# Moving the first layer's low weight parts from GpSimd to VectorE in an attention and two-MLP kernel

## The chip, the core and the metric

The kernel runs on one core of a Trainium2 chip. The core has a matrix engine (TensorE, PE in the profile), a vector engine (VectorE, DVE), a scalar engine (ScalarE, ACT), GpSimd (POOL) and a queue that issues DMAs (SyncE, SP). Each engine takes its own instructions in the order in which they were written, and waits where an operand of another engine or of a DMA isn't there yet. The metric is the device time of one execution in microseconds (us), measured in several runs; the profile is of one more execution of the same program.

## The reference

The program computes three things in a row: a linear attention with a feature map of exponentials, an MLP with a SiLU gate, and an MLP with a squared ReLU. Shapes: 4 batches, 8 heads, 576 tokens, head size 64, 128 features; then 2304 tokens, model width 512, hidden width 2048.

```python
def phi(x):
    proj = np.einsum('bhsd,df->bhsf', x, w_phi)
    proj = proj - np.max(np.abs(proj), axis=-1, keepdims=True)
    return np.concatenate([np.exp(proj), np.exp(-proj)], axis=-1)
q_p, k_p = (phi(q), phi(k))
kv = np.einsum('bhsf,bhsd->bhfd', k_p, v)
z = np.sum(k_p, axis=2)
num = np.einsum('bhsf,bhfd->bhsd', q_p, kv)
den = np.einsum('bhsf,bhf->bhs', q_p, z)[..., None] + 1e-06
x = (num / den)                       # [batch, heads, tokens, 64] -> [2304, 512]
h = x @ moe_w_in;  x = (h * (1.0 / (1.0 + np.exp(-h)))) @ moe_w_out
h = np.maximum(x @ moe2_w_in, 0.0);  out = (h * h) @ moe2_w_out
```

## The kernel before, in words

**Blocks and chunks.** The 2304 tokens are cut into 8 blocks of 288 (half a batch each). The hidden width of each MLP is cut into 16 chunks of 128. For a block i and a chunk c of layer L, `chunk` (line 871) multiplies the block's input by the chunk's input weights into a bank `h` (line 888, 12 matmuls), applies the activation on ScalarE and VectorE into tiles `a`, `gh`, `gl`, and adds the product with the chunk's output weights to four banks `o` (line 933, 12 matmuls). All 16 chunks of a block come before the next block; block 0 of layer 0 is therefore the place where each chunk's weights are used for the first time. They then stay in SBUF for the other seven blocks.

**Splits.** A matmul operand is not used as it is, but as a high part (rounded by a cast on ScalarE, `hi_act`, line 327) and a low part (the number less its high part, `lo_on`, line 331), and three products are added. Line 331 is one helper for all low parts; which engine runs it is an argument.

**Weights.** They come as float64 bits. For each half chunk (`part` 0 is the input half, 1 the output half) `w_conv` (line 394) loads 512 KB into one of three raw buffers (`wr`), takes the magnitude on ScalarE (line 408), and packs a float32 with four VectorE instructions (lines 414, 416, 420, 424) into `wc`. `w_split` (line 438) then makes the high part on ScalarE and the low part, both in the tile `w` of the chunk. In layer 0 the low part of half chunks 0 to 29 is made on GpSimd, and that of the last two on VectorE (`LP0, LP1 = 0, 2`, line 276, and line 1002). In layer 1 all are made on VectorE.

**Attention.** `keys_of` (line 479) makes the keys' features (`pk`, `kp`) and their product with the values (`pkv`, `kv`) for a batch and a pair of heads. `queries_of` (line 716) makes for half a batch and a pair of heads the projection (`pq`, evacuated to `qp`), its maximum over the 128 partitions on GpSimd (`peak`, line 763, into `qm`), the difference on VectorE (line 769), two exponentials on ScalarE (`qe`, line 781), the product with `kv` (`pn`, line 815), and the division by the denominator, whose reciprocals go through DRAM (`rr`, `rd`, `qb`). Names carry the numbers of the block and the pair: `qm1_2` is the maximum of block 1 and pair 2.

**The order.** No order is written by hand. `Plan` (line 65) plays the operations through with a cost for each and a key that says when it is wanted, and emits them in the order in which they start there: for every engine the ready operation with the least key. The costs are numbers of the program: `MM` and `MM256` (line 260) for a matmul, 450 + 6.25 S for a partition maximum (line 771), `pool(n)` (line 252) and `dve(n)` (line 248) for elementwise work on GpSimd and VectorE. A cost has no effect on the chip except through the order.

**GpSimd.** It runs a few memsets, the 32 partition maxima, and the 30 subtractions. In the program's order of GpSimd's instructions a row of kind ISA without a tile stands wherever the work turns from subtractions to maxima or back.

Of the kernel before, what the change touches and what calls it, by code (L numbers as in the profile page):

```python
# [17 lines left out]

B, H, S, D, F = 4, 8, 576, 64, 128
NTOK, DM, DFF = B * S, H * D, 2048  # L20
NP = H // 2          # pairs of heads
HB = S // 2          # tokens of a block: half a batch
NB = NTOK // HB      # blocks
NC = DFF // 128      # chunks of the hidden layer
ND = DM // 128
KT = 116             # tokens of a k tile; the last one has 112
NKT = 5
LAST = S - KT * (NKT - 1)
D1 = D + 1           # a head's values and a column of ones
RP, RN = 96, 2 * HB // 96  # L30


# [1 line left out]
    return struct.unpack("<f", struct.pack("<I", bits))[0]  # L34


# the high word of a float64, read as a float32: of float32's least and largest numbers
MIN_HI = float_of(896 << 20)
MAX_HI = float_of((1151 << 20) - 1)

# [7 lines left out]


class Buf:  # L50
    """A tile that a pool lends from its first writer to its last user."""

    def __init__(self, pool, make, unit):
        self.pool, self.make, self.unit, self.users, self.tile = pool, make, unit, 0, None


class Unit:
    """A chain of operations that shares the slots with others."""

    def __init__(self, n):  # L60
        self.n = n
# [1 line left out]


class Plan:
    """Operations in the order of the data, put by their costs into an order for the engines."""

    LAT = {"PE": 450, "SP": 150}
    DMA_LAT = 2000
# [1 line left out]
    def __init__(self, pools):  # L71
        self.ops, self.units, self.free = [], [], dict(pools)
        self.written, self.read, self.started = {"kvs": ()}, {}, set()
        self.last = {}       # pool -> [buffers to come back, pool that opens then, its size]

    def unit(self):
        u = Unit(len(self.units))
# [39 lines left out]
        return o  # L117

    def more(self, u, running):
        """The slots that unit `u` still needs beside those it holds, if it runs in its own order."""  # L120
        now = most = 0
        users = {}
        for o in u.ops:
            if o.state == 2:
                continue
            if o.state == 0 and o is not running:
                n = sum(b.pool == "t" for b in o.allocs)
                now += n
                most = max(most, now)
            for b in o.frees:  # L130
                if b.pool == "t":
                    users[b] = users.get(b, 0) + 1
                    if users[b] == b.users:
                        now -= 1
        return most

    def safe(self, o):
        """Whether the units can still end one after another once `o` has its buffers."""
        need = {}
        for b in o.allocs:  # L140
            need[b.pool] = need.get(b.pool, 0) + 1
        if any(self.free[pool] < n for pool, n in need.items()):
            return False
        n = need.get("t", 0)
        free = self.free["t"] - n
        if n and o.unit:
            for u in self.active:
                if u.n > o.unit.n:
                    break
                if u is not o.unit:  # L150
                    if self.more(u, None) > free:
                        return False
                    free += u.held
            if self.more(o.unit, o) > free:
                return False
        return True
# [100 lines left out]
    return max(600, kb * 1024 / 330.0)  # L257


MM, MM256 = 122, 109  # L260


@with_exitstack
def attention_then_two_mlps(ctx, tc, kT, qT, v, w_phi, w1, w2, out):
# [8 lines left out]
    WARM = 4  # L273
    JF, BX = 2, 1
    EW = 14
    LP0, LP1 = 0, 2
    NX, NXK = 1, 2      # batches whose queries, and keys, are multiplied as float32

    const = ctx.enter_context(tc.tile_pool(name="const", bufs=1))
    wp = ctx.enter_context(tc.tile_pool(name="wp", bufs=NC - NW))  # L280
# [5 lines left out]
    rp = ctx.enter_context(tc.tile_pool(name="rp", bufs=NRAW))  # L286
    tp = ctx.enter_context(tc.tile_pool(name="tp", bufs=NT))
    psb = ctx.enter_context(tc.tile_pool(name="psb", bufs=8, space=PSUM))
    # the space of the last chunks' weights serves the attention at the start
    early = tc.tile_pool(name="ep", bufs=NE)  # L290
    ep = [early.__enter__()]

# [15 lines left out]
    op = plan.op  # L308
# [13 lines left out]
            b.tile = b.make()  # L322
        return b.tile

    # ---- exact splits: hi has the 12 leading bits, lo the rest
    def hi_act(dst, src):
        nc.scalar.copy(out=dst, in_=src)  # L327

# [4 lines left out]
    def lo_cost(engine, n):  # L333
        return dve(n) if engine == "DVE" else pool(n)

    # ---- constants
    wbl = const.tile([128, 2, F], F32, name="wbl")
    wst_hi = const.tile([128, F], F32R, name="wst_hi")
    wst_lo = const.tile([128, F], F32R, name="wst_lo")
# [33 lines left out]
    op(T0 - 99, "ACT", 600, phi_hi, r=["wraw", "wbl0"], w=["phi_hi"])  # L373
    op(T0 - 99, "DVE", 600, phi_lo, r=["wraw", "phi_hi"], w=["phi_lo"])

    # the tensor engine's clock rises after a few microseconds of work
    blank_u = Buf("e", lambda: ep[0].tile([128, 256], F32, tag="t", name="zeros"), None)
    blank_ps = Buf("eb", lambda: psb.tile([128, 512], F32, tag="b", name="warm"), None)

# [7 lines left out]
    op(T0 - 100, "DVE", 300, zeros, w=["zeros"], bufs=[blank_u])  # L387
    op(T0 - 100, "PE", WARM * 850, warm, r=["zeros"], bufs=[blank_u, blank_ps])

    # ---- weights of a layer, chunk by chunk: [in hi, in lo, out hi, out lo].  # L390
    # They come as float64 bits: word 0 holds the low 32, word 1 the high 32.
    wch = {}

    def w_conv(layer, c, part, key):
        """float64 to float32: |x| is kept in float32's range, the exponent loses 896, and 3 bits
        of the low word follow the 20 mantissa bits of the high one."""
        n = f"{layer}_{c}_{part}"
        u = plan.unit()
        u.early = layer == 0 and 2 * c + part < EW
        raw = Buf("raw", lambda: rp.tile([128, 512, 2], I32, tag="raw", name="wr" + n), None)  # L400
        f = slot("wc" + n, u, (128, 512))

        def load():
            src = (w1, w2)[layer][c, :, part * 512:(part + 1) * 512].bitcast(I32)
            nc.sync.dma_start(out=get(raw).rearrange("p n two -> p (n two)"), in_=src)

        def mag():
            nc.scalar.activation(out=get(f), in_=get(raw)[:, :, 1].bitcast(F32), func=AF.Abs)  # L408

        def bits(i):  # L410
            t, b = get(f), get(f).bitcast(I32)
            lo, hi = get(raw)[:, :, 0], get(raw)[:, :, 1]
            if i == 0:
                nc.vector.tensor_scalar(out=t, in0=t, scalar1=MIN_HI, scalar2=MAX_HI, op0=ALU.max, op1=ALU.min)
            elif i == 1:
                nc.vector.tensor_scalar(
                    out=b, in0=b, scalar1=5, scalar2=2, op0=ALU.logical_shift_left, op1=ALU.logical_shift_right
                )
            elif i == 2:
                nc.vector.scalar_tensor_tensor(  # L420
                    out=b, in0=lo, scalar=29, in1=b, op0=ALU.logical_shift_right, op1=ALU.bitwise_or
                )
            else:
                nc.vector.scalar_tensor_tensor(  # L424
                    out=b, in0=hi, scalar=-(1 << 30), in1=b, op0=ALU.bitwise_and, op1=ALU.bitwise_or
                )

        k = ("wf", layer, c, part)
        hold = int(key) - 6 if layer else 0
        r = [(("c", 0, hold // NC, hold % NC), "h")] if layer else []  # L430
        op(key - 4, "SP", dma(512), load, r=r, w=[(k, 0)], bufs=[raw])
        op(key, "ACT", act(512), mag, r=[(k, 0)], w=[(k, 1)], bufs=[raw, f], unit=u)
        for i in range(4):
            op(key, "DVE", dve(512, i < 2), lambda i=i: bits(i), r=[(k, 1 + i)], w=[(k, 2 + i) if i < 3 else k],
               bufs=[raw, f], unit=u)
        return f, u
# [36 lines left out]
        op(key, "SP", dma(256), load, r=[(k, "d"), (("c", 0, NB - 1, max(c - 2, 0)), "h")], w=[k], bufs=[f], unit=u)  # L473
        return f, u

    # ---- keys and values of a pair of heads
    kvs = {}

    def keys_of(j, p, key, lo_engine="DVE"):
# [173 lines left out]
        ps = pkv  # L653

        def kv_mm():
            # a head's 65 columns of values and ones among 128, the others fall between the results
            for g, tiles in enumerate(groups):
                nt = KT if g < 2 else LAST
                for i, t in enumerate(tiles):
# [43 lines left out]
            op(key, "DVE", dve(4 * D1), kv_lo, r=[(K, "t"), (K, "kvh")], w=[(K, "kvl")], bufs=[ps, kv], unit=u)  # L703
        kvs[j, p] = kv

    # ---- queries of a pair of heads, half a batch
    xs = {}

    def x_buf(u):
# [6 lines left out]
    def queries_of(b, p, key, lo_engine="DVE"):  # L716
# [51 lines left out]
            f = get(pr).rearrange("p a t -> p (a t)")  # L768
            nc.vector.tensor_tensor(out=f, in0=f, in1=get(mx), op=ALU.subtract)  # L769

        op(key, "POOL", 450 + 6.25 * S, peak, r=[(Q, "pr", 0), (Q, "pr", 1)], w=[(Q, "m")], bufs=[pr, mx], unit=u)
        op(key, "DVE", dve(S), sub, r=[(Q, "m")], w=[(Q, "d")], bufs=[pr, mx], unit=u)
        hls = []
        for s in range(2):
# [48 lines left out]
            op(key, "ACT", act(HB, True), evac, r=[(Q, "n", a)], w=[(Q, "num", a)], bufs=[ps, num], unit=u)  # L823

        rb = slot("qb" + n, u, (D, 2, HB))
        # the denominators' reciprocals, spread over partitions, then one row for all of a head's
        rr = Buf("rr", lambda: sp.tile([RP, RN], F32, tag="rr", name="rr" + n), None)

        def spread():
# [35 lines left out]
        op(key, "ACT", act(HB), x_hi, r=[(Q, "x")], w=[("xh", b, p)], bufs=[x, xb])  # L865
        op(key, "DVE", dve(HB), x_lo, r=[(Q, "x"), ("xh", b, p)], w=[("xl", b, p)], bufs=[x, xb])

    # ---- the MLPs on blocks of HB tokens
    accs = {}

    def chunk(L, i, c, key):
# [108 lines left out]
            op(key, "DVE", dve(S), lo, r=[X] + [("xh", NB + i, d) for d in ps], w=[("xl", NB + i, d) for d in ps],  # L980
               bufs=[raw, xb], unit=u)

    # ---- the work in the order of the data, with keys: when it is wanted, in chunks of a block
    todo = []

    def want(key, f, *args):
        # what a block reads is declared before it, however late it is wanted
        first = key
        if f in (keys_of, queries_of):
            first = min(key, 32 * args[0] - P["qe"] - 1 if f is keys_of else 16 * args[0] - 0.5)  # L990
        if f == "key":
            first = min(key, args[1])
        todo.append((first, len(todo), key, f, args))
# [4 lines left out]
    for c in range(NC):  # L998
        def first(key, c=c):
            for part in range(2):  # L1000
                f, u = w_conv(0, c, part, key + 0.5 * part)
                w_split(0, c, part, f, u, key + 0.5 * part, "POOL" if LP0 <= 2 * c + part < 32 - LP1 else "DVE")
        want(min(T0 + P["w0"] + P["ws"] * c, c - P["we"]), "key", first, c - 1)
    for j in range(B):
        t = 32 * j
# [76 lines left out]
```

## Time and profile before

| what | value |
|---|---|
| three runs | 1100.44, 1100.52, 1101.17 us (median 1100.52) |
| profiled execution, first to last instruction (span) | 1099.0 us |
| the runs' median less that span | 1.5 us |
| PE, busy | 1016.9 us |
| DVE, busy | 619.4 us |
| ACT, busy | 549.3 us |
| POOL, busy | 117.7 us |

The page gives no other time of the profiled execution than its span; the 1.5 us are taken for what lies around it. An engine is busy while an instruction of it runs; an idle engine waits for another, and "<-" names what ended the wait. The clock column (PEclk) is the TensorE clock that was granted, as a share of full speed.

### The profile page before, as it was taken

The numbers are of one execution on the slowest core, as the hardware profiler recorded it, in microseconds if no ns is written. First come the engines' busy times: TensorE is split into PE (matmuls) and PEld (weight loads), VectorE is DVE, ScalarE is ACT, GpSimd is POOL, SyncE is SP. The second block draws the span as 40 slices with busy tenths as digits, with TensorE's granted clock in tenths as the row PEclk, the third lists the DMA queues.
The fourth block names the chain that finished last, engine by engine and source line by source line (L and its number), as shares of the span: only waits on it lengthen the run. The fifth ranks groups of instructions, "written<-read, shape, count | busy, mean of one in ns | idle before, by whom it ended". The sixth has DMA issues, their size and how long they took to land.

```text
span 1099.0 us, 19156 instructions
## 1 busy us (share of the span) xinstructions
PE 1016.9 (93%) x7424; PEld 988.3 (90%) x7424; DVE 619.4 (56%) x1248; ACT 549.3 (50%) x1369; POOL 117.7 (11%) x86
## 2 busy tenths in 40 slices
PE   7855299599999999999999999999999999999998
PEld 6624198599999999899999999999999999999998
DVE  4555389657666675678999768633333232323232
ACT  4453268566768765777766456332323232323222
POOL 2223243223000320002011000000000000000000
PEclk8967599899999999999999999999999999999999
DMA  6342335302230022424455587201001010100000
GB/s 169 101 124 69 97 95 171 96 29 60 65 78 23 23 77 56 106 89 137 131 188 159 167 283 245 85 1 45 17 28 37 9 44 1 44 1 23 1 23 22
DMA packets 67387, 88.39 MB, mean 80 GB/s; under 512 B 30816, under 2 KB 43232, under 8 KB 67296
## 3 DMA queue, kind: packets, MB, share of 16 engines
q1 hardware_dynamic: 67296, 87.17, 26.7%
q8 instruction: 58, 0.95, 0.4%
q14 instruction: 33, 0.27, 0.1%
HBM read 69.17 MB, written 17.90 MB: 79 GB/s over the span
## 4 chain that ended last, share of the span: by engine, by line
PE 75%; DMA 7%; DVE 6%; issue 4%; ACT 3%; SPq 2%; POOL 2%; ACTq 0%; DVEq 0%; POOLq 0%
PE h L888 33%; PE o L933 33%; PE pn L815 4%; DMA wr<-w 2%; PE pkv L622 2%; PE pkv L665 1%; DMA v<-v 1%; POOL qm L763 1%; DVE wc L420 1%; DVE wc L424 1%; PE pk L561 1%; SPq L503 1%; DMA rd<-rr 1%; POOL w L331 1%; SPq L731 1%
## 5 line engine op out<-in xcount | busy, mean ns | idle before, releaser
L888 PE MATMUL h<-x,w 128*128 128x288 f32 x3072 | 453.3, 297 | 32.5 <-POOL w L331 31.8
L933 PE MATMUL o<-gh,w 128*128 128x288 f32 x2048 | 457.4, 297 | 1.4 <-ACT gh L327 1.4
L888 PEld LDWEIGHTS h<-x,w 128*128 128x128 f32 x3072 | 424.9, 190 | 35.7 <-POOL w L331 33.8
L933 PEld LDWEIGHTS o<-gh,w 128*128 128x128 f32 x2048 | 345.7, 189 | 2.2 <-ACT gh L327 1.7
L933 PE MATMUL o<-gl,w 128*128 128x288 f32 x1024 | 302.9, 296 | 0.5 <-DVE gl L331 0.5
L331 DVE TENSOR_TENSOR gl<-a,gh 128x288 fp32r<-128x288 f32 x256 | 120.3, 470 | 146.5 <-ACT gh L327 145.4
L327 ACT CAST gh<-a 128x288 fp32r<-128x288 f32 x256 | 111.9, 437 | 181.4 <-PE o L933 148.0
L933 PEld LDWEIGHTS o<-gl,w 128*128 128x128 f32 x1024 | 193.5, 189 | 1.3 <-DVE gl L331 0.9
L905 DVE TENSOR_TENSOR a<-h,a 128x288 f32<-128x288 f32 x128 | 58.4, 456 | 108.1 <-ACT a L896 108.1
L896 ACT ACTIVATE a<-h 128x288 f32<-128x288 f32 x128 | 52.6, 411 | 117.3 <-PE h L888 117.1
L763 POOL PARTITION_ALL_REDUCE qm<-qp x32 | 70.3, 2216 | 326.5 <-ACT qp L756 262.5
L901 DVE SCALAR_TENSOR_TENSOR a<-a,h 128x288 f32<-128x288 f32 x128 | 57.4, 449 | 54.6 <-ACT a L894 53.6
L894 ACT ACTIVATE a<-h 128x288 f32<-128x288 f32 x128 | 53.4, 418 | 42.6 <-PE h L888 42.5
L781 ACT ACTIVATE qe<-qp 128x576 f32<-128x576 f32 x64 | 41.9, 682 | 37.4 <-DVE qp L769 30.2
L331 POOL TENSOR_TENSOR w<-wc,w 128x512 fp32r<-128x512 f32 x30 | 45.3, 1520 | 91.5 <-ACT w L327 45.4
L408 ACT ACTIVATE wc<-wr 128x512 f32<-128x512 f32 x64 | 43.3, 679 | 13.4 <-DMA wr<-w 13.0
L815 PE MATMUL pn<-qe,kv 128*65 128x288 f32 x64 | 23.8, 534 | 25.9 <-ACT qe L781 25.9
L420 DVE SCALAR_TENSOR_TENSOR wc<-wr,wc 128x512 int32<-128x512 int32 x64 | 46.5, 729 | 0.8
L424 DVE SCALAR_TENSOR_TENSOR wc<-wr,wc 128x512 int32<-128x512 int32 x64 | 45.7, 715 | 0.3
L769 DVE TENSOR_TENSOR qp<-qp,qm 128x576 f32<-128x576 f32 x32 | 26.8, 840 | 33.1 <-POOL qm L763 33.1
L594 ACT ACTIVATE ke<-pk,mx 116x128 f32<-116x128 f32 (+1 forms) x160 | 45.3, 386 | 0.0
L665 PEld LDWEIGHTS pkv<-v,kp 116*128 116x128 f32 (+1 forms) x320 | 38.0, 198 | 7.1 <-ACT kp L649 5.4
(84 smaller groups left out, 1009.8 us busy)
## 6 DMA issues: line engine op xcount, KB each, us to landing
wr<-w SPq DMA_DIRECT2D x64, 512.0 KB, 4.3
w2d<-wc SPq DMA_DIRECT2D x32, 256.0 KB, 2.9
w2f<-w2d SPq DMA_DIRECT2D x32, 256.0 KB, 3.6
qr<-qT SPq DMA_DIRECT2D x56, 144.0 KB, 3.1
v<-v SPq DMA_DIRECT2D x16, 290.0 KB
kr<-kT SPq DMA_DIRECT2D x16, 288.0 KB, 4.8
qb<-rd SPq DMA_DIRECT2D x32, 144.0 KB, 4.0
x2d<-y SPq DMA_DIRECT2D x32, 144.0 KB, 1.8
```

Of the source, the lines that this page charges most:

```text
L327: nc.scalar.copy(out=dst, in_=src)
L331: e.tensor_tensor(out=dst, in0=src, in1=hi.bitcast(F32), op=ALU.subtract)
L420: nc.vector.scalar_tensor_tensor(out=b, in0=lo, scalar=29, in1=b, op0=ALU.logical_shift_right, op1=ALU.bitwise_or)
L424: nc.vector.scalar_tensor_tensor(out=b, in0=hi, scalar=-(1 << 30), in1=b, op0=ALU.bitwise_and, op1=ALU.bitwise_or)
L763: nc.gpsimd.partition_all_reduce(get(mx), get(pr).rearrange("p a t -> p (a t)"), 128, bass.bass_isa.ReduceOp.absmax)
L815: nc.tensor.matmul(get(ps)[:D1, :HB], w, get(e)[:, t], start=x == 0, stop=x == len(ops) - 1)
L888: nc.tensor.matmul(get(ps)[:, :HB], a, x[:, cc], start=k == 0, stop=k == 3 * ND - 1)
L894: nc.scalar.activation(out=a, in_=get(ps)[:, :HB], func=AF.Tanh, scale=0.5)
L896: nc.scalar.activation(out=a, in_=get(ps)[:, :HB], func=AF.Relu)
L901: nc.vector.scalar_tensor_tensor(out=a, in0=a, scalar=1.0, in1=get(ps)[:, :HB], op0=ALU.add, op1=ALU.mult)
L905: nc.vector.tensor_tensor(out=a, in0=get(ps)[:, :HB], in1=a, op=ALU.mult)
L933: nc.tensor.matmul(get(acc)[:, :HB], a, g, start=c == 0 and x == 0, stop=c == NC - 1 and x == 2)
```

## The change

The low parts of all 32 half chunks of layer 0 are now subtracted on VectorE. `LP0` and `LP1` go, comments go, and three costs of the planner are other numbers: a matmul 132 in place of 122, one of 256 columns 117 in place of 109, a partition maximum 2250 in place of 4050 (450 + 6.25 · 576). Lines after 276 move up by one.

```diff
-MM, MM256 = 122, 109
+MM, MM256 = 132, 117
...
-    LP0, LP1 = 0, 2
...
-        op(key, "POOL", 450 + 6.25 * S, peak, r=[(Q, "pr", 0), (Q, "pr", 1)], w=[(Q, "m")], bufs=[pr, mx], unit=u)
+        op(key, "POOL", 2250, peak, r=[(Q, "pr", 0), (Q, "pr", 1)], w=[(Q, "m")], bufs=[pr, mx], unit=u)
...
-                w_split(0, c, part, f, u, key + 0.5 * part, "POOL" if LP0 <= 2 * c + part < 32 - LP1 else "DVE")
+                w_split(0, c, part, f, u, key + 0.5 * part, "DVE")
```

On GpSimd, at the place where the maxima of blocks 0 and 1 stand between the first weights' low parts, the order before was (`qm` a maximum, `w` a low part, `v` a memset of ones):

```order
L763 ISA
L763 ISA qm0_2_395<-qp0_2_385 128x576
L763 ISA qm0_3_467<-qp0_3_426 128x576
L508 MEMSET v1_0_521 116x10
L331 ISA
L331 TENSOR_TENSOR w0_1_366<-wc0_1_1_374,w0_1_366 128x512
L763 ISA
L763 ISA qm1_0_552<-qp1_0_529 128x576
L331 ISA
L331 TENSOR_TENSOR w0_2_563<-wc0_2_0_497,w0_2_563 128x512
L331 TENSOR_TENSOR w0_2_563<-wc0_2_1_526,w0_2_563 128x512
L763 ISA
```

and is now:

```order
L762 ISA qm0_2_405<-qp0_2_383 128x576
L762 ISA qm0_3_466<-qp0_3_449 128x576
L507 MEMSET v1_0_492 116x10
L762 ISA qm1_0_548<-qp1_0_503 128x576
L507 MEMSET v1_1_564 116x10
L762 ISA qm1_1_623<-qp1_1_578 128x576
L762 ISA qm1_2_659<-qp1_2_621 128x576
L762 ISA qm1_3_682<-qp1_3_669 128x576
```

The low parts and the tile-less ISA rows between maxima are gone: in the whole program 15 such rows at lines 763 and 331 before, one now, ahead of the first maximum.

On VectorE, in block 0 of layer 0, the conversion of chunk 6 stood before among the activations (`a`, `gl`) like this:

```order
L420 SCALAR_TENSOR_TENSOR wc0_6_0_728<-wr0_6_0_694,wc0_6_0_728 128x512
L414 TENSOR_SCALAR wc0_6_1_808<-wc0_6_1_808 128x512
L424 SCALAR_TENSOR_TENSOR wc0_6_0_728<-wr0_6_0_694,wc0_6_0_728 128x512
L331 TENSOR_TENSOR gl0_0_2_805<-a0_0_2_803,gh0_0_2_804 128x288
L901 SCALAR_TENSOR_TENSOR a0_0_3_853<-a0_0_3_853,h0_0_3_789 128x288
L416 TENSOR_SCALAR wc0_6_1_808<-wc0_6_1_808 128x512
L414 TENSOR_SCALAR wc0_7_0_858<-wc0_7_0_858 128x512
L420 SCALAR_TENSOR_TENSOR wc0_6_1_808<-wr0_6_1_735,wc0_6_1_808 128x512
L331 TENSOR_TENSOR gl0_0_3_855<-a0_0_3_853,gh0_0_3_854 128x288
L424 SCALAR_TENSOR_TENSOR wc0_6_1_808<-wr0_6_1_735,wc0_6_1_808 128x512
```

and stands now with its low parts (`w0_6`) among them:

```order
L423 SCALAR_TENSOR_TENSOR wc0_6_0_776<-wr0_6_0_728,wc0_6_0_776 128x512
L415 TENSOR_SCALAR wc0_6_1_848<-wc0_6_1_848 128x512
L330 TENSOR_TENSOR gl0_0_4_882<-a0_0_4_880,gh0_0_4_881 128x288
L419 SCALAR_TENSOR_TENSOR wc0_6_1_848<-wr0_6_1_800,wc0_6_1_848 128x512
L330 TENSOR_TENSOR w0_6_899<-wc0_6_0_776,w0_6_899 128x512
L900 SCALAR_TENSOR_TENSOR a0_0_5_912<-a0_0_5_912,h0_0_5_867 128x288
L423 SCALAR_TENSOR_TENSOR wc0_6_1_848<-wr0_6_1_800,wc0_6_1_848 128x512
L413 TENSOR_SCALAR wc0_7_0_885<-wc0_7_0_885 128x512
L330 TENSOR_TENSOR gl0_0_5_914<-a0_0_5_912,gh0_0_5_913 128x288
L415 TENSOR_SCALAR wc0_7_0_885<-wc0_7_0_885 128x512
L330 TENSOR_TENSOR w0_6_899<-wc0_6_1_848,w0_6_899 128x512
```

Each low part stands here four rows behind the last packing step (line 424, now 423) of its half chunk. TensorE's order in blocks 0 and 1 keeps the same tiles in nearly the same places. On VectorE nine of the low parts stand ahead of the last low part of block 0's input, and 23 behind it.

## Rows read from the trace of the kernel before

**Rows 1.** The profile's page: busy time of PE, and TensorE in 40 equal slices of the span (27.5 us each), busy share and granted clock in tenths.

```profile
PE 1016.9 (93%) x7424; PEld 988.3 (90%) x7424; DVE 619.4 (56%) x1248; ACT 549.3 (50%) x1369; POOL 117.7 (11%) x86
...
PE   7855299599999999999999999999999999999998
...
PEclk8967599899999999999999999999999999999999
```

**Rows 2.** Busy time of each engine in four stretches that cover the span: start and end (us), length, then PE, PEld, DVE, ACT, POOL busy us (instructions), granted clock, DMA share, GB/s. The first stretch ends where the first MLP matmul starts, the second where block 0's last weights are there.

```profile
0.00:95.10 95.10, 61.78 (x289) 44.28 (x289) 45.85 (x96) 44.79 (x97) 23.53 (x25) 0.77 0.42 114
95.10:226.00 130.90, 91.58 (x603) 83.76 (x602) 88.98 (x165) 69.60 (x195) 42.79 (x30) 0.85 0.38 111
226.00:660.00 434.00, 429.34 (x3262) 426.30 (x3261) 321.52 (x643) 293.69 (x749) 51.41 (x31) 1.00 0.36 106
660.00:1099.00 439.00, 434.17 (x3277) 433.93 (x3275) 163.07 (x347) 141.24 (x329) 0.00 (x0) 1.00 0.12 39
```

**Rows 3.** The waits of PE in 0 to 226 us: waiting line, what it waited for, us in total, times, longest.

```profile
PE h L888 <- POOL w L331: 31.8, 4, 17.9
PE pn L815 <- ACT qe L781: 25.9, 3, 12.9
PE pkv L665 <- ACT kp L649: 5.2, 1, 5.2
```

**Rows 4.** GpSimd's timeline: start us, us, instruction, and in brackets the idle time ahead of it. These are six of the 14 changes between the two kinds of work up to 228 us, the longest and the shortest gap among them.

```profile
37.78 3.75 POOL L331 TENSOR_TENSOR w<-wc,w 128x512 fp32r<-128x512 f32 x3 [7.84 <-issue]
...
69.57 2.15 POOL L763 PARTITION_ALL_REDUCE qm<-qp  x1 [6.77 <-issue]
...
87.83 2.16 POOL L763 PARTITION_ALL_REDUCE qm<-qp  x1 [5.79 <-issue]
...
134.86 4.98 POOL L331 TENSOR_TENSOR w<-wc,w 128x512 fp32r<-128x512 f32 x4 [7.12 <-issue]
...
209.42 2.16 POOL L763 PARTITION_ALL_REDUCE qm<-qp  x1 [5.81 <-ACT w L327]
218.31 2.49 POOL L331 TENSOR_TENSOR w<-wc,w 128x512 fp32r<-128x512 f32 x2 [6.74 <-issue]
```

**Rows 5.** The same view later, where only maxima are left on GpSimd.

```profile
361.81 6.40 POOL L763 PARTITION_ALL_REDUCE qm<-qp  x3 [64.00 <-ACT qp L756]
```

**Rows 6.** PE's timeline at the places where it waited longest.

```profile
73.35 4.10 PE L815 MATMUL pn<-qe,kv 128*65 128x288 f32 x8 [8.99 <-ACT qe L781]
...
91.61 4.10 PE L815 MATMUL pn<-qe,kv 128*65 128x288 f32 x8 [12.90 <-ACT qe L781]
...
136.17 3.25 PE L888 MATMUL h<-x,w 128*128 128x288 f32 x12 [17.95 <-POOL w L331]
...
141.53 1.75 PE L888 MATMUL h<-x,w 128*128 128x288 f32 x12
```

**Rows 7.** The waits of VectorE in the first stretch, 0 to 95.1 us.

```profile
DVE qp L769 <- POOL qm L763: 25.5, 3, 11.8
```

**Rows 8.** The waits of VectorE in the second stretch, 95.1 to 226 us.

```profile
DVE a L901 <- ACT a L894: 28.7, 2, 18.5
DVE qp L769 <- POOL qm L763: 5.5, 1, 5.5
```

**Rows 9.** The instructions that touch the weight tiles `w`: count, then shortest, median and longest ns. The first row is layer 1's low part, the second layer 0's.

```profile
L331 DVE TENSOR_TENSOR w<-w2f,w x32: 682/685/693, 646.8 to 704.0; 128x512 fp32r<-128x512 f32 x32
L331 POOL TENSOR_TENSOR w<-wc,w x30: 1252/1290/3089, 37.8 to 219.5; 128x512 fp32r<-128x512 f32 x30
```

**Rows 10.** The packing instructions of VectorE from 0 to 225 us, with GpSimd's subtractions beside them: count, busy us, mean ns, idle before.

```profile
L424 DVE SCALAR_TENSOR_TENSOR wc<-wr,wc 128x512 int32<-128x512 int32 x32 | 23.8, 747 | 0.2
L420 DVE SCALAR_TENSOR_TENSOR wc<-wr,wc 128x512 int32<-128x512 int32 x32 | 23.6, 744 | 0.4
L416 DVE TENSOR_SCALAR wc<-wc 128x512 int32<-128x512 int32 x32 | 15.6, 494 | 0.2
L414 DVE TENSOR_SCALAR wc<-wc 128x512 f32<-128x512 f32 x32 | 15.1, 477 | 7.5 <-ACT wc L408 7.4
```

**Rows 11.** The same forms from 225 to 500 us, without subtractions on GpSimd.

```profile
L420 DVE SCALAR_TENSOR_TENSOR wc<-wr,wc 128x512 int32<-128x512 int32 x4 | 2.8, 689 | 0.1
...
L424 DVE SCALAR_TENSOR_TENSOR wc<-wr,wc 128x512 int32<-128x512 int32 x3 | 2.1, 684 | 0.0
...
L414 DVE TENSOR_SCALAR wc<-wc 128x512 f32<-128x512 f32 x4 | 1.7, 424 | 2.7 <-ACT wc L408 2.7
L416 DVE TENSOR_SCALAR wc<-wc 128x512 int32<-128x512 int32 x4 | 1.7, 421 | 0.0
```

**Rows 12.** VectorE's timeline at the start of the maximum that stands at 209.42 us in rows 4: one of the two low parts that VectorE already makes in layer 0.

```profile
209.42 1.83 DVE L331 TENSOR_TENSOR w<-wc,w 128x512 fp32r<-128x512 f32 x1
```

**Rows 13.** Two stretches in which GpSimd makes nothing but subtractions and memsets; columns as in rows 2.

```profile
137.40:165.00 27.60, 27.47 (x184) 25.76 (x183) 23.43 (x43) 19.02 (x54) 12.18 (x9) 0.94 0.32 97
165.00:192.00 27.00, 24.30 (x176) 22.30 (x175) 24.77 (x45) 22.45 (x73) 8.89 (x6) 1.00 0.58 169
```

**Rows 14.** The raw weights: waits for them from 0 to 225 us (us, times, longest), and the time from a load's issue to its landing in the whole span (shortest, median, longest).

```profile
ACT wc L408 <- DMA wr<-w: 8.6, 6, 3.7
...
DMA to landing us min/median/max: 3.5/4.3/7.6
```

**Rows 15.** The longest wait of PE after 225 us.

```profile
PE pkt L691 <- ACT ke L594: 1.9, 1, 1.9
```

## The prediction

> **What bounds the kernel now.** The first view is the page's busy line and its slices [rows 1]. PE is busy for 1016.9 of 1099.0 us, so at most 82.1 us can come from idle time of PE, and the slices show where it lies: six of the first eight are far from full, most of these have a lowered clock, and nearly all later ones are at nine tenths. The second view, four stretches of the span, puts numbers to that [rows 2]. To 95.1 us PE idles for 33.3 us, from there to 226.0 for 39.3, and in the whole 873 us behind it for 4.7 + 4.8. So whatever the change does for the better, it does before 226 us. What stands behind that is bound by the matmuls themselves.
>
> The third view is who PE waits for before 226 us [rows 3]: 31.8 us for GpSimd's low weight parts, 25.9 for the queries' exponentials (`qe`), 5.2 for an exponential of keys (`kp`), 62.9 in all. Only the first names GpSimd. The fourth view, GpSimd's timeline, shows that the other two are its doing too [rows 4]. GpSimd works for 23.5 + 42.8 us in these stretches [rows 2], which is little, but ahead of each of the 14 changes between subtractions and maxima it stands idle for 5.8 to 7.8 us, often with "issue" as the reason: no engine is waited for. Where maxima follow maxima there is no such gap: three take 6.40 us together [rows 5]. At 87.83 us a maximum ends such a gap of 5.79 us, and PE's wait of 12.90 us ends at 91.61 us with the exponentials of that maximum; at 134.86 us a subtraction ends one of 7.12 us, and PE's longest wait, 17.95 us, ends at 136.17 [rows 4, 6]. The program's order has a tile-less ISA row at each change, so I read the gap as the price of the change of work, not of an instruction.
>
> VectorE tells the same from its side: in the first stretch it waits 25.5 us for maxima [rows 7], in the second 5.5 for maxima and 28.7 for activations of matmuls that PE couldn't start [rows 8].
>
> **The change, part by part.** *Removed:* 30 subtractions of 1.25 us or more on GpSimd [rows 9] and the 14 changes with their gaps. GpSimd then has some 11 maxima of 2.2 us in the first two stretches; it can take each as soon as `qp` is there. What is late next is VectorE: it has 45.9 of 95.1 and 89.0 of 130.9 us busy already [rows 2].
>
> *Added:* 30 subtractions on VectorE. The same form in layer 1 takes 0.685 us [rows 9], so 20.6 us. In the new order nine of the 32 low parts stand before block 0's input is complete, and 23 behind, of which two were VectorE's before: 9 x 0.685 = 6.2 us for the first stretch, 21 x 0.685 = 14.4 for the second. Each waits for its high part's cast on ScalarE. Behind it VectorE holds the activations, for which PE's `o` matmuls wait, and the differences of `qp`, for which the exponentials and `pn` wait. The cover is what lies between the last packing step and the low part: three instructions at the place shown, and a packing step alone is 0.42 to 0.69 us [rows 11]. Were the cover gone and each low part kept waiting for its own length, it would cost up to another 20.6 us.
>
> *The sum goes by VectorE.* First stretch: 95.1 - 25.5 + 6.2 = 75.8 us. Second: 130.9 - 28.7 - 5.5 + 14.4 = 111.1 us. I let all waits for maxima and for the late matmuls go, and keep VectorE's other idle time, 23.7 and 7.7 us, as it is.
>
> *Contention, both ways.* With subtractions on GpSimd the four packing steps take 747, 744, 494 and 477 ns, without them 684, 689, 421 and 424 [rows 10, 11]. That is 0.244 us for a half chunk, and 7.8 us over 32, which come back. Against it stand the maxima that VectorE now meets while it is busy. A low part that began with a maximum took 1.83 us instead of 0.685 [rows 9, 12], 1.14 more. None of 11 so hit costs nothing, all 11 cost 12.6; I take six of them, 6.9 us, since VectorE is busy for most of the time but not only with such instructions. Net: -0.9.
>
> The Trainium skill, "SBUF — State Buffer", section "Who interferes with whom", speaks against the change here: a VectorE instruction with two SBUF inputs and a GpSimd instruction that reads SBUF exclude each other, and the loser is blocked for the whole of the other. The trace agrees that there is a block, but 1.83 us is less than a maximum of 2.16 and a subtraction of 0.685 one after the other, so by the row it is shorter than the rule has it. By the rule the 11 maxima would cost up to 23.8 us.
>
> *Moved at no cost:* the planner's costs for matmuls and maxima change nothing but the order. TensorE's keeps its tiles in nearly the same places in blocks 0 and 1, under the same waits. Behind 226 us there are 4.7 us of idle to gain before the last stretch [rows 2], and the longest single wait there is 1.9 us [rows 15]; five new ones would cost about 10. I take 0. The raw loads on the SP queue keep their number but come closer together; so far ScalarE waited for them 8.6 us in all [rows 14].
>
> Total: 75.8 + 111.1 - 0.9 = 186.0 us where 226.0 were, 40.0 less. 1099.0 - 40.0 = 1059.0 us of span, and with the 1.5 us by which the runs' median lies above the profiled span, 1060.5 us.
>
> How tight is that? VectorE would be busy for about 89.0 + 14.4 = 103.4 of 111.1 us in the second stretch, 93%. In the two stretches without a change on GpSimd it reached 23.43 of 27.60 (85%) and 24.77 of 27.00 (92%), while PE was at 99 and 90% [rows 13]. At 85% the stretch would take 121.6 us, 10.5 more; at 100%, 7.7 less. So the likeliest case's own range is about 1050 to 1072.
>
> **The rivals.**
> *PE stays the bound.* If VectorE's idle time closes up too, PE gets all its 62.9 us back: 1100.5 - 62.9 = 1037.6. For it: PE's work before 226 us is 61.8 + 91.6 = 153.4 us [rows 2], some of it at a lowered clock (12 matmuls took 3.25 us behind the long wait, 1.75 soon after [rows 6]). Against it: VectorE's sum above is 33 us longer. Chance 0.08.
>
> *VectorE is blocked by each maximum for its whole length.* All 11 cost 2.16 us in place of my 6.9 us together: 1060.5 + 16.9 = 1077.4. Beside the skill's rule stands only that the row shows half as much. Chance 0.12.
>
> *The gap belongs to maxima and not to the change.* Then the changes don't go away with the subtractions, PE still waits for `qe` and `kp`, and only the 31.8 us come back, against up to 20.6 us of new work on VectorE: 1068.7 to 1089.3, the middle 1079. Against it: three maxima in a row without a gap [rows 5], and gaps before subtractions of the same size [rows 4]. Chance 0.08.
>
> *Slower: the raw loads become the chain.* Three buffers hold the raw weights, and a buffer is free only when VectorE has run the last packing step. With low parts in VectorE's order those steps come later relative to the work, so the next load is issued later; 22 loads fall in the second stretch, and a load lands after 4.3 us in the median [rows 14]. If half of that were exposed at each, 22 x 2.15 = 47.3 us would go, more than the 40.0 gained: 1107.8. It decides from about 1.8 us per load. Against it: in the kernel before the exposed part was 8.6 us for 32 loads, about 0.3 each, and that in 226 us of which VectorE was idle for 91. Chance 0.05.
>
> **How the numbers follow.** My forecast, 1060.5 with 1050 to 1072, has 0.65; the rivals in turn 0.08, 0.12, 0.08 and 0.05; 0.02 is left for no change by some sum of small things. A measurement of this kernel can tell about 0.2%, 2.2 us, from no change; all cases but the last two lie far below that, so faster has 0.93, the same 0.02, slower 0.05. The range 1040 to 1082 holds the forecast, the blocking case and more than half of the third rival; it leaves out the first and the slower one, no change, and the third's tail, some 0.18.
>
> **What would show it.** On the new profile GpSimd's timeline must have no idle ahead of maxima that stands without a releaser, and the first MLP matmul should start near 76 us in place of 95.09, block 0's last weights be there near 186 in place of 226. PE's waits there should name VectorE's low parts or ScalarE behind them, some 30 to 40 us in all where 72.6 were idle. VectorE should be above 85% busy between the two marks, and its packing steps back at 0.69 and 0.42 us, apart from those beside a maximum. I would be wrong if the gaps before maxima remain, if ScalarE waits for raw loads much beyond 8.6 us, if VectorE's instructions beside maxima grow by 2 us each, or if PE has new idle time behind 226 us beyond the 9.5 us of before.

## The result

The changed kernel takes 1062.63 us (median of four runs, 1062.18 to 1063.95); the kernel before took 1100.85 beside it. The ratio is 0.9645 with a 95% interval of 0.963 to 0.966, so 38.2 us or 3.5% less. Forecast were 1060.5 us, with a range of 1040 to 1082.

The page of the kernel after, the lines that answer to [rows 1]:

```profile
span 1060.4 us, 19152 instructions
PE 1019.5 (96%) x7424; PEld 992.0 (94%) x7424; DVE 629.7 (59%) x1278; ACT 550.0 (52%) x1369; POOL 75.6 (7%) x56
...
PE   7879798998999999999999999999999999999998
...
PEclk8989988999999999999999999999999999999999
```

PE's work is the same; the slices of 2 and 5 tenths among the first eight are gone, and the granted clock of the two early stretches is higher: 0.86 and 0.90 below, 0.77 and 0.85 in [rows 2]. PE's idle time is 40.9 us in place of 82.1.

The four stretches, the first two cut at the same events as in [rows 2] (columns as there): the first MLP matmul, and block 0's last weights.

```profile
0.00:74.70 74.70, 60.21 (x289) 43.72 (x289) 49.15 (x95) 42.02 (x91) 19.08 (x22) 0.86 0.54 142
74.70:186.40 111.70, 96.77 (x612) 88.97 (x611) 97.33 (x198) 75.88 (x205) 8.00 (x6) 0.90 0.44 132
186.40:620.00 433.60, 427.01 (x3244) 424.01 (x3243) 318.92 (x639) 289.85 (x743) 48.56 (x29) 1.00 0.36 106
620.00:1060.40 440.40, 435.53 (x3288) 435.30 (x3286) 164.30 (x350) 142.27 (x331) 0.00 (x0) 1.00 0.12 39
```

The events now come at 74.7 and 186.4 us where they came at 95.1 and 226.0: 20.4 us are won in the first stretch and 19.2 in the second. Behind them the program takes 874.0 us, where it took 873.0. (The marks are round: the last low part itself ends at 225.1 us before and at 186.2 now, which leaves 873.9 and 874.2 behind it.)

GpSimd's timeline, beside [rows 4]:

```profile
16.57 2.15 POOL L762 PARTITION_ALL_REDUCE qm<-qp  x1 [7.36 <-DVE kd L571]
...
42.07 2.14 POOL L762 PARTITION_ALL_REDUCE qm<-qp  x1 [10.98 <-DMA wr<-w]
46.07 2.32 POOL L762 PARTITION_ALL_REDUCE qm<-qp  x1 [1.86 <-DMA qb<-rd]
...
70.51 4.74 POOL L762 PARTITION_ALL_REDUCE qm<-qp  x2 [5.25 <-ACT qp L755]
...
174.22 2.32 POOL L762 PARTITION_ALL_REDUCE qm<-qp  x1 [4.39 <-ACT qp L755]
177.27 2.14 POOL L762 PARTITION_ALL_REDUCE qm<-qp  x1 [0.74 <-ACT qp L755]
```

GpSimd still idles, but the idle time ends with the evacuation of `qp` by ScalarE, that is with its input, and where inputs come close together so do the maxima. (Two of these rows name a DMA, but there too ScalarE's copies of `qp` ended 0.09 us before, at 41.98 and 45.98 us.) Only ahead of the first maximum, where the one tile-less ISA row is left, stand 7.36 us, 3.3 of them after its `qp` was there at 13.26. No floor of 5.8 us stands ahead of the others any more.

The waits of PE up to 186.4 us, the longest four (us, times, longest), beside [rows 3]:

```profile
PE pn L814 <- ACT qe L780: 5.6, 1, 5.6
PE o L932 <- ACT gh L326: 3.4, 2, 2.0
PE pk L560 <- DMA kr<-kT: 2.7, 2, 2.5
PE pn L814 <- ACT kv L675: 2.6, 1, 2.6
```

Where three rows made 62.9 us, no row is above 5.6. Most of the time is spread over waits for ScalarE, VectorE and input DMAs, and none is for GpSimd.

### The profile page after: what moved, and what is told of

Same layout as the page of the kernel before. It is cut to its first block, busy times and chain, and to the rows that moved or that the text cites. A ratio compares the mean times of both kernels' runs of the same rounds, so it can differ in the third digit from the quotient of the medians.

```text
span 1060.4 us, 19152 instructions
## 1 busy us (share of the span) xinstructions
PE 1019.5 (96%) x7424; PEld 992.0 (94%) x7424; DVE 629.7 (59%) x1278; ACT 550.0 (52%) x1369; POOL 75.6 (7%) x56
## 4 chain that ended last, share of the span: by engine, by line
PE 74%; DMA 10%; DVE 10%; ACT 3%; issue 2%; SPq 1%; POOL 0%; ACTq 0%; DVEq 0%
PE h L887 32%; PE o L932 32%; DMA wr<-w 3%; PE pn L814 3%; PE pkv L621 2%; DMA qb<-rd 2%; PE pkv L664 1%; DVE wc L419 1%; DVE wc L423 1%; DMA rd<-rr 1%; PE pk L560 1%; ACT kp L634 1%; DMA rr<-qn 1%; DVE x L852 1%; SPq L502 1%
## 5 line engine op out<-in xcount | busy, mean ns | idle before, releaser
L326 ACT CAST gh<-a 128x288 fp32r<-128x288 f32 x256 | 111.7, 437 | 199.0 <-PE o L932 148.7
L762 POOL PARTITION_ALL_REDUCE qm<-qp x32 | 73.1, 2303 | 319.2 <-ACT qp L755 178.7
L664 PEld LDWEIGHTS pkv<-v,kp 116*128 116x128 f32 (+1 forms) x320 | 41.1, 210 | 1.4 <-issue 0.6
L814 PE MATMUL pn<-qh,kv 128*65 128x288 f32 x192 | 41.8, 294 | 0.0
L664 PE MATMUL pkv<-v,kp 116*128 116x128 f32 (+1 forms) x320 | 41.4, 293 | 0.0
L413 DVE TENSOR_SCALAR wc<-wc 128x512 f32<-128x512 f32 x64 | 28.9, 454 | 19.3 <-ACT wc L407 18.9
```

Source lines behind the costliest of these rows:

```text
L664: nc.tensor.matmul(get(ps)[:, o:o + 128], get(kps[2 * g + s])[:nt, 2 * i + a], get(vt)[:nt, c:c + 128], start=t == 0 and a == 0 and s == 0 ...
L762: nc.gpsimd.partition_all_reduce(get(mx), get(pr).rearrange("p a t -> p (a t)"), 128, bass.bass_isa.ReduceOp.absmax)
L814: nc.tensor.matmul(get(ps)[:D1, :HB], w, get(e)[:, t], start=x == 0, stop=x == len(ops) - 1)
```

## The experiments

Theory A is the prediction's: the change of work on GpSimd costs some 6.8 us each time, these gaps made PE wait, and without them VectorE sets the pace up to block 0's last weights. Rival B: what cost was the subtractions' own length on GpSimd. Rival C: the planner's truer costs made a better order. All ratios are against the kernel before, run on the same chip.

**1. The costs alone.** The kernel before, with two lines of the change:

```diff
-MM, MM256 = 122, 109
+MM, MM256 = 132, 117
...
-        op(key, "POOL", 450 + 6.25 * S, peak, r=[(Q, "pr", 0), (Q, "pr", 1)], w=[(Q, "m")], bufs=[pr, mx], unit=u)
+        op(key, "POOL", 2250, peak, r=[(Q, "pr", 0), (Q, "pr", 1)], w=[(Q, "m")], bufs=[pr, mx], unit=u)
```

> The kernel before with the three new planner costs alone; the low parts stay on GpSimd, whose order now has 16 changes between subtractions and maxima where it had 14. Theory A (the changes of work on GpSimd, about 6.8 us each, made the waits; the costs matter little): 1095 to 1115 us. Rival C (the truer costs brought the gain through a better order): 1080 us or less.

Measured: 1123.27 us, ratio 1.0198 (1.0172 to 1.0224), slower, and more so than either theory said. GpSimd's timeline, and PE's behind it, before the first MLP matmul:

```profile
91.53 2.15 POOL L763 PARTITION_ALL_REDUCE qm<-qp  x1 [5.82 <-issue]
100.83 2.50 POOL L331 TENSOR_TENSOR w<-wc,w 128x512 fp32r<-128x512 f32 x2 [7.14 <-ACT x L327]
109.17 2.15 POOL L763 PARTITION_ALL_REDUCE qm<-qp  x1 [5.85 <-issue]
...
112.95 3.88 PE L815 MATMUL pn<-qe,kv 128*65 128x288 f32 x8 [13.54 <-ACT qe L781]
116.44 6.78 PE L888 MATMUL h<-x,w 128*128 128x288 f32 x48
```

Eight changes now stand ahead of the first MLP matmul, where six stood, and it starts 21.3 us later (95.09 before). Block 0's last low part ends 10.3 us later, at 235.4, and what follows takes 883.8 us where it took 873.9. So about half of the loss stands behind the last weights, where both orders have one change left; what makes it there was not tested. Rival C falls: with the old place of the low parts the new costs lose 21 us.

**2. The move alone.** The changed kernel with the old costs.

```diff
-MM, MM256 = 132, 117
+MM, MM256 = 122, 109
...
-        op(key, "POOL", 2250, peak, r=[(Q, "pr", 0), (Q, "pr", 1)], w=[(Q, "m")], bufs=[pr, mx], unit=u)
+        op(key, "POOL", 450 + 6.25 * S, peak, r=[(Q, "pr", 0), (Q, "pr", 1)], w=[(Q, "m")], bufs=[pr, mx], unit=u)
```

> The changed kernel with the three old planner costs: the low parts on VectorE, no change of work on GpSimd after the first maximum. Theory A: 1058 to 1070 us, near the changed kernel's 1062.6. Rival C: 1085 to 1100, since the costs are those of before.

Measured: 1057.86 us, ratio 0.9603 (0.9578 to 0.9627). The move of the low parts brings the whole gain; with it, too, the new costs lose about 0.4%. The order is another one: the last low part ends only at 189.8 us, but behind it the program takes 865.5 us, 8.7 less than the changed kernel.

**3. The changes of work without the work.** One column is subtracted on GpSimd ahead of each of the first eight maxima (its result is overwritten by the maximum):

```diff
         def peak():
+            if b < 2:
+                x = get(pr)
+                nc.gpsimd.tensor_tensor(out=get(mx)[:, :1], in0=x[:, 0, :1], in1=x[:, 0, 1:2], op=ALU.subtract)
             nc.gpsimd.partition_all_reduce(
```

> The changed kernel with a subtraction of one column on GpSimd ahead of each of the first eight maxima: it takes some 0.1 to 0.3 us itself, and its result is overwritten by the maximum. VectorE keeps all low parts. Theory A: 15 gaps of 5.8 to 7.8 us come back on GpSimd, about 13.5 us for each maximum, and the time rises to 1095 to 1140. Rival B (the length of GpSimd's subtractions and the work queued behind them made the waits, not the change): no gaps, 1060 to 1067.

Measured: 1101.55 us, ratio 1.0002 (0.9986 to 1.0017): the time of the kernel before, to the measurement's error. GpSimd's timeline:

```profile
28.12 0.18 POOL L764 TENSOR_TENSOR qm<-qp 128x1 f32<-128x1 f32 x1 [6.79 <-ACT wc L407]
35.63 2.15 POOL L765 PARTITION_ALL_REDUCE qm<-qp  x1 [7.32 <-issue]
46.50 0.19 POOL L764 TENSOR_TENSOR qm<-qp 128x1 f32<-128x1 f32 x1 [8.60 <-ACT qp L755]
54.32 2.15 POOL L765 PARTITION_ALL_REDUCE qm<-qp  x1 [7.63 <-DVE mx L565]
63.65 0.18 POOL L764 TENSOR_TENSOR qm<-qp 128x1 f32<-128x1 f32 x1 [7.17 <-issue]
69.89 2.15 POOL L765 PARTITION_ALL_REDUCE qm<-qp  x1 [6.06 <-issue]
```

Subtractions of 0.18 us (two of the eight took 0.69 and 1.49) bring back gaps of 6.06 us and more on both sides, but for the very first, though VectorE keeps all low parts. This is the run that settles the cause: the gap belongs to the change between the two kinds of instruction, and PE waits for it. Rival B falls, and so does the prediction's third rival, that it belongs to maxima: the gaps stand before the subtractions too, though nothing that these read was made on GpSimd, and in the changed kernel maxima start 0.74 and 1.86 us after the work before them.

That the time is just that of before is chance. The stretches of this run, cut at its first MLP matmul and at the end of its last low part:

```profile
0.00:113.03 113.03, 67.00 (x289) 46.32 (x289) 46.98 (x101) 42.59 (x94) 16.80 (x26) 0.78 0.36 97
113.03:224.80 111.77, 96.91 (x610) 88.67 (x609) 97.17 (x192) 74.14 (x201) 13.01 (x9) 0.88 0.42 129
```

All 38 us are lost in the first stretch, where the kernel before lost 20.4; the second is as short as in the changed kernel. So this run shows what the changes cost through the maxima. The 19.2 us of the second stretch, where PE waited for low parts that stood behind a change, are read from [rows 3, 4, 6]; experiment 5 bears that reading out.

**4. VectorE's share doubled.** Layer 0's low parts are made twice.

```diff
         def lo():
-            lo_on(engine, get(w)[:, 2 * part + 1], get(f), get(w)[:, 2 * part])
+            for _ in range(1 if layer else 2):
+                lo_on(engine, get(w)[:, 2 * part + 1], get(f), get(w)[:, 2 * part])
```

> The changed kernel with each of layer 0's 32 low parts made twice on VectorE, the planner's costs as they are. If VectorE sets the pace to the end of block 0, as the prediction's sum has it: 32 x 0.69 = 22 us more work, of which 15 to 22 show, 1077 to 1085. If the raw loads or PE set it: less than 8 us more, under 1071.

Measured: 1076.34 us, ratio 0.9774 (0.975 to 0.9797), 13.7 us over the changed kernel. That lies between the two expectations: of 22 us more work on VectorE, 62% show. They don't show evenly. The first MLP matmul starts at 76.36 us, where it started at 74.69: VectorE spends 7.5 us more on low parts before it, and 1.7 show. From there to the end of the last low part, at 199.5 us in place of 186.2, it spends 16.6 us more, and 11.6 show. VectorE sets most of the pace in the second stretch, but little of it in the first.

**5. The middle low parts back on GpSimd.** Between the maxima of block 1 and those of block 2 GpSimd has nothing to do but memsets. The low parts of half chunks 12 to 25 fall there, so they can stand in one piece.

```diff
-                w_split(0, c, part, f, u, key + 0.5 * part, "DVE")
+                w_split(0, c, part, f, u, key + 0.5 * part, "POOL" if 12 <= 2 * c + part < 26 else "DVE")
```

> The changed kernel with the low parts of half chunks 12 to 25 back on GpSimd: in its order they stand in one piece between the maxima of block 1 and those of block 2, so only two changes of work are added. Theory A (changes cost, subtractions don't; VectorE now sets the pace): VectorE loses 14 x 0.69 = 9.6 us of work and gets back 14 x 0.24 = 3.4 of contention, so 3 to 7 us less than the changed kernel's 1062.6: 1055 to 1060. Rival B (the subtractions on GpSimd are what made PE wait): 1068 or more.

Measured: 1054.29 us, ratio 0.9561 (0.9538 to 0.9584): 8 us less than the changed kernel, the fastest here, and 0.7 below what theory A allowed. GpSimd's timeline at the two changes:

```profile
71.00 4.74 POOL L762 PARTITION_ALL_REDUCE qm<-qp  x2 [4.80 <-ACT qp L755]
94.87 2.06 POOL L330 TENSOR_TENSOR w<-wc,w 128x512 fp32r<-128x512 f32 x1 [19.13 <-ACT w L326]
...
156.21 1.63 POOL L330 TENSOR_TENSOR w<-wc,w 128x512 fp32r<-128x512 f32 x1 [6.48 <-ACT w L326]
169.55 2.69 POOL L762 PARTITION_ALL_REDUCE qm<-qp  x1 [11.71 <-ACT qp L755]
```

GpSimd idled for 19.13 and 11.71 us at these places for want of input, and began 0.09 and 0.21 us after ScalarE had made it (at 94.78 and 169.34 us), so a change of some 7 us is hidden in each. The subtractions themselves are harmless there: the second stretch takes 104.4 us with 14 of them on GpSimd, 7 less than with none, which speaks against rival B in that stretch too.

**6. The same with the old costs.** Both edits, that of experiment 2 and that of 5.

> As the kernel with the middle low parts on GpSimd, but with the planner's three old costs, which alone gave 1057.9 with all low parts on VectorE. Theory A: the two gains add, 1050 to 1056. If the gain by the old costs hangs on that very order: 1056 to 1064.

Measured: 1067.86 us, ratio 0.9687 (0.9661 to 0.9713), a miss of both expectations: worse than either edit alone. Block 0's last weights are there at the same time as in experiment 5 (179.8 and 179.4 us). The loss comes behind them. The longest waits of PE from 180 to 620 us:

```profile
PE h L887 <- ACT x L326: 10.9, 2, 6.4
PE pq L751 <- DVE ql L330: 1.8, 3, 0.8
```

Twice, until 591.5 and 600.7 us, a piece of a block's input, which the attention makes, isn't there when PE wants it.

**7 and 8. A fourth raw buffer.** It needs SBUF, so two work tiles go, and a control has the two tiles less and three buffers.

```diff
-    NT, NRAW, NATT, NG, NU = 14, 3, 2, 3, 4
+    NT, NRAW, NATT, NG, NU = 12, 4, 2, 3, 4
```

> The changed kernel with 12 work tiles in place of 14, the control for the next run. All theories: 1061 to 1070.

> The same with four raw buffers in place of three. If VectorE alone sets the pace up to block 0's last weights: within 2 us of the control with 12 work tiles. If the raw loads share in it (ScalarE now waits 25.8 us for them up to 190 us, where it was 8.6): 4 to 10 us less than that control.

Measured: the control 1074.07 us, ratio 0.9736 (0.9706 to 0.9767), more than expected; with four buffers 1070.10, ratio 0.9701 (0.9674 to 0.9728), 4.0 less, which is the least that was expected if the loads share in the pace. The intervals overlap, so the time doesn't decide. In the traces the last weights' low part starts at 170.16 us in place of 177.87, which is what that theory wants. The first MLP matmul starts at 64.61 in place of 74.09, but that is no gain: six run, and the seventh waits for block 0's input.

```profile
64.61 1.06 PE L887 MATMUL h<-x,w 128*128 128x288 f32 x6
74.24 0.61 PE L887 MATMUL h<-x,w 128*128 128x288 f32 x1 [8.56 <-ACT x L326]
```

PE's two longest rows of waits in these stretches are

```profile
PE h L887 <- DVE w L330: 9.9, 2, 8.5
PE h L887 <- ACT x L326: 9.4, 2, 8.6
```

where the control has 6.2 us for `w` and no such row for `x`. The planner also makes another order for four buffers. So that the raw loads share in the pace is likely from the last weights' place, but not shown. What the fourth buffer alone would bring without the loss of two tiles stays open, since it doesn't fit.

**9 and 10. The two costs apart.** The changed kernel with the old cost of matmuls alone, then with the old cost of maxima alone.

> The changed kernel with the old cost of a matmul (122 and 109) and the new one of a maximum. All three old costs gave 1057.9, all three new ones 1062.6. If the matmul's cost makes that difference: 1056 to 1060. If the maximum's does: 1061 to 1065. If each new order is its own case: outside both.

> The changed kernel with the old cost of a maximum (4050) and the new ones of matmuls. If the maximum's cost makes the difference: 1056 to 1060. If the matmul's does: 1061 to 1065. If each new order is its own case: outside both.

Measured: 1064.95 us (ratio 0.9657, 0.9643 to 0.9672) and 1073.10 (0.9731, 0.9713 to 0.9748). With all old costs it was 1057.86, with all new 1062.63. The first result alone would have put the difference down to the cost of maxima; the second, outside both ranges, refutes that. The effects don't add: each set of costs makes its own order, and its time falls where it falls between 1058 and 1073. Which cost is "right" can't be read from that.

## Why the prediction was right

**The place.** All the gain came before block 0's last weights, and the time behind them changed by 1 us at most.

**The gaps.** That they were the price of the change of work was read from three rows: idle time without a releaser, maxima in a row without a gap [rows 5], and PE's waits ending with the work behind a gap [rows 4, 6]. Experiment 3 shows it directly for the maxima; for the low parts of the second stretch the reading of these rows stands, with experiment 5 beside it.

**VectorE's sum.** It gave 75.8 us for the first stretch and, with contention, 110.2 for the second; measured are 74.7 and 111.7, together 186.4 against 186.0. Inside the second stretch two terms were off and cancel: VectorE is busy for 97.3 us where the working had 103.4, and idle for 14.4 where 7.7 of other idle time were kept. So it is at 87%, between the 85 and 92% of [rows 13], not at 93. That it is the pace there is borne out by experiment 4, for some seven tenths. In the first stretch it isn't: VectorE is busy for 49.15 of 74.7 us, and of more work on it only 1.7 of 7.5 us showed. The 75.8 us came out because the waits for maxima went and the other idle time stayed (25.6 us, kept at 23.7), not because VectorE was full. That the whole sum came within 0.4 us is therefore luck in part; that it came near is not. What sets the rest of the pace was not taken apart.

**Contention.** Six of 11 maxima were to hit a VectorE instruction for 1.14 us each, 6.9 in all. Up to 186.4 us seven do, for 0.8 to 1.1 us each, and four more VectorE instructions grow by 0.2 to 0.7, some 8.7 us in all. These rows of VectorE's timeline stand beside the pair of maxima at 70.51 us and the one at 177.27:

```profile
70.29 0.69 DVE L330 TENSOR_TENSOR w<-wc,w 128x512 fp32r<-128x512 f32 x1
70.89 1.78 DVE L419 SCALAR_TENSOR_TENSOR wc<-wr,wc 128x512 int32<-128x512 int32 x1
72.60 0.65 DVE L413 TENSOR_SCALAR wc<-wc 128x512 f32<-128x512 f32 x1
73.17 1.77 DVE L423 SCALAR_TENSOR_TENSOR wc<-wr,wc 128x512 int32<-128x512 int32 x1
...
177.33 1.55 DVE L330 TENSOR_TENSOR gl<-a,gh 128x288 fp32r<-128x288 f32 x1
```

The two packing steps take 1.78 and 1.77 us instead of the 0.69 of [rows 11], 1.1 more. The last row, which takes 0.46 undisturbed, ends at 178.88 us, before its maximum does (179.41, as far as GpSimd's spans can be trusted). The second rival, a block for a maximum's whole length, falls: none of the seven lost more than 1.1 us to a maximum of 2.1 to 2.6. The Trainium skill ("SBUF — State Buffer", section "Who interferes with whom") has the loser blocked for the whole of the other instruction; these rows show a shorter block.

**The raw loads.** One of the prediction's own signs of being wrong came true, and the sum held all the same. ScalarE's wait for raw weights up to 190 us:

```profile
ACT wc L407 <- DMA wr<-w: 25.8, 15, 4.1
```

It was 8.6 [rows 14]. VectorE's wait behind it didn't grow, though: 6.6 us, where it was 7.4 [rows 10]. So the mechanism of the slower rival is there, but little of it reaches the path, and a longer wait of ScalarE was no good sign of it.

**The costs.** This step was too sure of itself: the new costs were taken as 0, with 4.7 to gain and 10 to lose. In the changed kernel they lose 4.8 us by experiment 2, and in the kernel before 21 by experiment 1. The sum came out well because it was made from the trace of before, stretch by stretch, and an order that is worse by 0.4% is within what its terms were off. That this order was not one that loses 10 us (experiment 10) was not foreseen, and is luck.

**What was left over.** PE's idle time up to 186.4 us is 29.4 us, at the lower edge of the 30 to 40 forecast, spread over many short waits; rows that name ScalarE make 14.6 us of it, those that name VectorE's low parts 2.5. How much of ScalarE's share lies behind low parts was not taken apart. The 2 us by which the time lies above the forecast are, by the marks used here, 1.0 behind the last weights, 0.4 before them, and 0.7 by which the median lies further above the profiled span than it did.

## What to carry to other kernels

An engine that is idle 89% of the time can still be what everything waits for: look at the idle time ahead of its instructions, and whether a gap of much the same size, often without a releaser, stands wherever its kind of work changes. Then group the work of a kind, or move one kind away; a piece that stays must lie where the engine has nothing to do for longer than the gap. And when an order is planned from costs, a change of a cost is an edit of its own: measure it apart from the one that is meant.

## What was not expected

Truer costs didn't make a better order: with the move in place, four sets of costs gave 1057.9, 1062.6, 1065.0 and 1073.1 us, and the best set for all low parts on VectorE was the worse one of two with the middle ones on GpSimd (1067.9 against 1054.3). A spread of 1.4% between orders of the same work is four tenths of the whole gain of 3.5% here.
